# Two transposes of the last batch on TensorE, and three units one product later: a retention and Fourier-mixing block on one Trainium2 core

## The chip, the cores and the metric

The kernel runs on one core of one Trainium2 chip. The metric is the device time of one execution in microseconds. Before the change the median of 3 runs is 237.1 us (237.0 to 237.59). A difference of about 0.3% is what such a measurement can tell from none.

The core's engines run side by side, each through its own list of instructions: TensorE (PE in the profile, with its weight loads as PEld), VectorE (DVE), ScalarE (ACT), GpSimd (POOL) and SyncE (SP), whose queue here issues nearly all DMA. They wait for one another by semaphores.

## The reference

A retention layer over 4 batches, 8 heads, 768 steps and head size 64, and then a Fourier mixer with a feed-forward block of 512 to 2048 to 512:

```python
for t in range(S):
    state = gamma[None, :, None, None] * state + np.einsum('bhd,bhe->bhde', k[:, :, t], v[:, :, t])
    y[:, :, t] = scale * np.einsum('bhd,bhde->bhe', q[:, :, t], state)
...
x = np.ascontiguousarray(attn_out.transpose(0, 2, 1, 3)).reshape(B, S, H * D)
...
X = np.fft.fft(x, axis=1)
X = np.fft.fft(X, axis=2)
mixed = np.real(X).astype(np.float32)
u = x + mixed
mu = np.mean(u, axis=-1, keepdims=True)
var = np.mean((u - mu) ** 2, axis=-1, keepdims=True)
un = (u - mu) / np.sqrt(var + 1e-06)
ch = np.maximum(un @ w_ch1, 0.0) @ w_ch2
return (u + ch).astype(np.float32)
```

## The kernel before

The sequence of 768 is cut into six blocks of 128. Retention is computed by blocks for pairs of heads (four pairs a batch): products inside a block with a decay mask, and a state carried from block to block. The Fourier transforms are products with cosine and sine tables after folds. The feed-forward block runs on row blocks of 128 rows; its first product needs the normalised rows transposed.

**The order.** The work is written as small units in two strings of names, `FIRST` (batch 0 up to its first normalised rows, with the front of its feed-forward) and `LATER` (the rest, lines 49 to 95). The loop at line 1465 calls the units of `LATER` in turn through `held` (line 188), which ties each instruction to the one before it on the same engine:

```python
for n in range(n0, len(ins)):
    m = n - 1
    while m >= 0 and ins[m].engine != ins[n].engine:
        m -= 1
    if m >= 0:
        tc.add_manual_dep(ins[n], ins[m].name,
```

So the place of a name in the string is its place in the order of every engine that it uses, the DMA queue of SP among them. Semaphores and the banks of the PSUM pools are assigned by the compiler. `ps_g` (line 135) has five banks and serves nearly all intermediate products; the feed-forward products have a pool of three.

**The names that matter here.** The digits after the kind are mostly batch, then pair or row block, then part; a letter after @ is the engine that evacuates.

- `cq`, `ck`, `cv` (lines 477, 493, 504): GpSimd casts q, k and v of a pair to half precision, k with its decay. The loads `l`, `lq`, `lk`, `lv` are issued on SP.
- `s b i half` (`kv_unit`, line 728): three or two products of k and v on TensorE; block 0 is copied by ScalarE (L744), the others are added to the state by VectorE (L746), one after the other. It needs `ck` and `cv`.
- `t b i` (`t_unit`, line 666): TensorE transposes q (six blocks, L677) and, for pairs 0 and 1, k (six more); ScalarE copies q in two halves (L682) and k (L687). For pairs 2 and 3 the k transpose is a DMA. It needs `cq` and `ck`.
- `a b i part` (`a_unit`, line 703): two products of kT and qT (L712), evacuated by VectorE with the mask (L716) or by ScalarE in two activations (L722) with a GpSimd select behind them (L724).
- `y b i h` (L760, L763): the output of one head from qT, the state, the masked products and v.
- `c b rt rb3 part` (`ch_unit`, line 1200): four of the sixteen products of the second feed-forward layer of batch 0 (L1206); it needs the activations of its four hidden blocks.
- `r b rt` (`rstd_unit`, line 1134): ScalarE's square root (L1140) and VectorE's reciprocal (L1142) for three row blocks of batch 0, or two of a later batch. `r00` first computes the mean and variance of row block 0 on VectorE (L1015, L1016).
- `x b kb` (`s2_unit`): the last Fourier product of a row block (L1071), two ScalarE copies, and the sums on VectorE (L1078, L1087); `X` adds the input on GpSimd (L1110, L1112); `n` takes the statistics on VectorE (L1121, L1122); `u` writes the normalised rows `un` on ScalarE (L1130) or GpSimd.
- `U b kb @ engine` (`unT_unit`, line 1145): the transpose of `un` into `unT`. With @d it is one DMA transpose on SP (L1149). With @v or @a TensorE transposes four 128x128 blocks (L1153) into a bank of `ps_g` and VectorE or ScalarE copies them (L1154):

```python
if eng == "d":
    nc.sync.dma_start_transpose(unT[:, :, kb * P:(kb + 1) * P], un)
    return
```

- `H b g n` (`hp_unit`, line 1251): in batches 1 to 3 the first feed-forward product of two row blocks 2g and 2g+1 together (L1259), so it needs `unT` of both; the relu is L1164 on ScalarE or L1161 on VectorE.
- `j`, `p`, `q` (lines 1268, 1290, 1313): the second layer of such a pair of row blocks as seven products of halves (Strassen): sums of halves on VectorE (L1277), products `p` (L1308), and the additions `q` to the result (L1322), after which a row block is stored.

Of the kernel before, what the change touches and what calls it, by code (L numbers as in the profile page):

```python
# [51 lines left out]

|
i02 U01@v x04 X04 x03 i10 U02@a x05 i13 X05 i12 K0 cq10 Z c0000 c0001 i22 i20 i03 i11 X03 l10
l11 l12 i21 ck10 cv10 cq11 ck11 n04 u04@a c0002 n05 i23 n03 t10 c0020 s100 c0021 cv11 s101 t11
r00 a100@a c0010 a102@v a101@v l13 cq12 s110 ck12 c0011 u05@a a111@v u03@a c0022 a110@a y100
a112@v V10 y101 t12 lq20 s111 TB c0003 c0012 y110 U05@a cv12 s120 cq13 c0013 U04@v U03@a y111
ck13 t13 c0023 O01 pz00 w10 lk20 h016@a cv13 O00 a120@v a121@a pz01 s121 a122@a s130 h01C@a
h012@a s131 a132@v cq20 a131@a y121 h015@a lv20 lq21 lk21 a130@v y120 tq20 V00 ck20 tk20 h018@a
y131 y130 lv21 cv21 O02 cv20 h017@a h010@a h014@a h01F@a h01E@a h011@a h013@a h019@a ck21 V11  # L60
fs10 h01D@a fs11 h01A@a fd10 fd11 g10 fe10 fe11 z1 h01B@v c0100 pz10 V01 a201@v c0110 f110@a
f100@a w30 f101@a cq21 w11 pz11 lq22 lk22 lv22 f111@a gr12@a gr11@a lq23 lk23 c0101 g112 w20
a202@a r01 c0102 s200 c0103 tk21 gr10@v x11@v X11 x10@v n11 X10 c0111 c0112 tq21 x12@v n10 cq22
lv23 w31 s201 a200@a u11@a s210 c0120 c0121 c0122 u10@g gr13@a c0123 x13@v ck23 O03 y200 y201
c0113 tq22 U11@a X12 U10@v O05 n12 X13 ck22 w21 tk22 cv23 x15@v s211 cq23 r10 O04 a211@a H101@s
H105@s a212@a a210@v H106@a s230 x14@v cv22 n13 H102@s lq30 H103@a H100@a H107@a j10104 y210
# [19 lines left out]
p221 q221 j22204 p224 j22248 p225 p226 j22448 q225 j22404 j22304 u30@g U30@d gr30@a q226 p222  # L86
q222 X32 j22348 gr31@a x34@v p223 p227 q227 x33@v X33 q223 n33 H301@a x35@v H303@s H300@a H302@b
H305@s u33@a j30104 j30204 H304@a H306@a j30304 n32 r30 H307@b p301 q301 j30148 j30348 j30248
u32@a U32@d p304 U33@d j30448 p305 q305 j30404 p306 q306 X34 p302 q302 p303 q303 p307 H312@s
H317@a q307 H311@v n34 X35 n35 H315@a H313@s H316@v H310@a j31104 j31304 H314@b j31148 r31  # L90
j31248 p311 q311 j31204 j31448 j31404 j31348 p314 p315 q315 u35@a U35@d u34@g U34@d p316 q316
p312 q312 p313 q313 p317 q317 H325@b H324@v H326@s H322@b H321@b H320@s j32103 H323@a H327@s
j32136 j32236 p321 j32336 j32436 r32 j32168 j32368 p322 p324 j32268 p325 j32303 q321 j32203 p326
j32468 j32403 q325 p323 q326 q322 q323 p327 q327
# [1408 lines left out]
```

## Time and profile before

| | |
|---|---|
| median of 3 runs | 237.1 us |
| profiled execution, its own time | 237.41 us |
| its span, first to last instruction | 235.7 us |
| granted TensorE clock, mean | 0.996 |
| ScalarE relu of the first layer (L1164) | 117 instructions, 51.2 us |
| DMA share, SP queue (hardware_dynamic) | 67.5% of 16 engines over the span |
| transposes of `un` by DMA (L1149) | 15 |
| transposes of `un` by TensorE (L1153) | 32, eight row blocks |

A row of a timeline gives the start in us from the span's start, the duration, the engine, the line, the operation, out and in, shapes and a count of merged instructions; the bracket is the time that the engine sat idle before and who released it. Ends of products on TensorE are modelled, so that they overlap the next start; starts tell more. SPq is the SP queue issuing a DMA; a DMA row in the chain of waits runs from issue to landing.

### The profile page before, as it was taken

To read this page: it belongs to the slowest core of one execution; us is meant where nothing else is said; L and a number is where in the kernel's file an instruction comes from. 1 tells how busy PE (TensorE), PEld (TensorE's weight loads), DVE (VectorE), ACT (ScalarE), POOL (GpSimd) and SP (SyncE) were. 2 spreads that over 40 slices of the span, in tenths; PEclk is the share of its full clock that TensorE was granted. 3 is DMA by queue.
4 is the path that set the end of the run, shared out by engine and by line. 5 is a ranking of instruction groups with operands and counts; after the bars stand their busy time and mean duration, and the time that the engine had idled before them with its cause. 6 is when DMAs were issued, how large, how long until landed. Compare 5 with 4: busy or idle time off the path is not lost. (4 is left out here: it accounts for less than half of the span.)

```text
span 235.7 us, 6275 instructions
## 1 busy us (share of the span) xinstructions
PE 220.4 (94%) x2407; PEld 179.0 (76%) x2407; DVE 197.5 (84%) x491; ACT 150.5 (64%) x383; POOL 102.6 (44%) x176
## 2 busy tenths in 40 slices
PE   0888999989999999999999999999999999899993
PEld 0366778866675556889988999989799888788892
DVE  8799884878799989999999999889997987659473
ACT  5989758569998636795847847758537456041330
POOL 8378802576560399939007569441004341010000
PEclk9999999999999999999999999999999999999998
DMA  7999999999999999999997959942102420402202
GB/s 176 236 268 242 237 207 207 211 217 234 195 270 203 238 208 205 188 252 198 255 215 140 219 101 185 127 89 96 40 3 90 46 90 0 116 21 45 92 0 92
DMA packets 100958, 36.84 MB, mean 156 GB/s; under 512 B 91457, under 2 KB 97985, under 8 KB 100929
## 3 DMA queue, kind: packets, MB, share of 16 engines
q1 hardware_dynamic: 96704, 32.25, 67.5%
q0 software_dynamic: 4224, 4.19, 10.8%
q8 instruction: 19, 0.31, 0.6%
q14 instruction: 11, 0.08, 0.1%
HBM read 27.26 MB, written 6.29 MB: 142 GB/s over the span
## 5 line engine op out<-in xcount | busy, mean ns | idle before, releaser
L1164 ACT ACTIVATE ht<-psh 128x256 f16<-128x256 f32 (+2 forms) x117 | 51.2, 467 | 38.9 <-PE psh L1259 37.0
L1259 PE MATMUL psh<-unT,w 128*128 128x256 f16 x576 | 66.8, 273 | 1.1 <-DMA unT<-un 1.1
L1259 PEld LDWEIGHTS <-w 128*128 128x128 f16 x576 | 55.3, 98 | 7.9 <-DMA unT<-un 1.5
L1308 PEld LDWEIGHTS <-ht 128*128 128x128 f16 x440 | 41.5, 98 | 6.5 <-ACT ht L1164 1.3
L1110 POOL TENSOR_TENSOR u<-u,x 128x256 f32<-128x256 f32 x21 | 13.5, 643 | 36.6 <-DVE u L1078 24.9
L1308 PE MATMUL ps<-wide,ht 128*128 128x256 f16 x216 | 27.8, 273 | 0.1
L1277 DVE TENSOR_TENSOR ht<-ht 128x512 f16<-128x512 f16 (+2 forms) x57 | 23.8, 433 | 3.8 <-ACT ht L1164 3.3
L724 POOL TENSOR_SCALAR_AFFINE_SELECT atm<-atm 128x512 f16<-128x512 f16 x25 | 15.9, 650 | 18.7 <-issue 11.7
L1206 PE MATMUL psc<-w,ht 128*128 128x512 f16 x96 | 23.6, 379 | 0.0
L499 POOL TENSOR_SCALAR kd<-k,gexp 128x384 f16<-128x384 f32 x22 | 14.1, 650 | 16.2 <-PE ps L915 12.4
L746 DVE SCALAR_TENSOR_TENSOR s<-s,gk,wkK 128x128 f16<-128x128 f16 x48 | 16.2, 343 | 4.8 <-ACT s L744 3.2
L722 ACT ACTIVATE atm<-wkA 128x256 f16<-128x256 f32 x50 | 15.8, 395 | 5.3 <-PE wkA L712 5.1
L1308 PE MATMUL ps<-w,ht 128*128 128x256 f16 x144 | 18.7, 273 | 0.4 <-ACT ht L1164 0.4
L1322 DVE SCALAR_TENSOR_TENSOR ob<-ps,stats,u 128x256 f32<-128x256 f32 (+2 forms) x27 | 15.0, 562 | 3.3 <-PE ps L1308 3.3
L1161 DVE TENSOR_SCALAR ht<-psh 128x512 f16<-128x512 f32 (+2 forms) x19 | 10.7, 566 | 7.3 <-ACT ht L1164 3.5
L1121 DVE BATCH_NORM_STATS2 bst<-u 128x6 f32<-128x512 f32 x21 | 14.3, 682 | 2.3 <-POOL u L1112 2.3
L1130 ACT ACTIVATE un<-u,stats 128x512 f16<-128x512 f32 x18 | 13.0, 728 | 4.5 <-DVE stats L1122 4.5
L1322 DVE SCALAR_TENSOR_TENSOR u<-ps,stats,u 128x256 f32<-128x256 f32 (+2 forms) x27 | 15.0, 562 | 0.6 <-PE ps L1308 0.6
L508 POOL TENSOR_SCALAR v<-v 128x768 f16<-128x768 f32 x11 | 10.1, 925 | 11.5 <-DMA v<-in_v_dram 11.5
L1206 PEld LDWEIGHTS <-ht 128*128 128x128 f16 x96 | 8.8, 98 | 7.3
L1112 POOL TENSOR_TENSOR u<-u,x 128x256 f32<-128x256 f32 x21 | 13.7, 652 | 0.0
L770 ACT ACTIVATE x<-wkY,gexp 128x384 f16<-128x384 f32 x24 | 13.1, 589 | 0.7 <-PE wkY L763 0.6
(225 smaller groups left out, 458.3 us busy)
## 6 DMA issues: line engine op xcount, KB each, us to landing
out_dram<-ob SPq DMA_DIRECT2D x23, 256.0 KB, 2.9
k<-in_k_dram SPq DMA_DIRECT2D x14, 384.0 KB, 5.6
v<-in_v_dram SPq DMA_DIRECT2D x14, 384.0 KB, 6.2
q<-in_q_dram SPq DMA_DIRECT2D x12, 384.0 KB, 5.3
w<-in_moe_w_ch_dram POOLq DMA_DIRECT2D x8, 512.0 KB, 10.9
wide<-in_q_dram SPq DMA_DIRECT2D x4, 384.0 KB, 6.1
wide<-in_v_dram SPq DMA_DIRECT2D x2, 384.0 KB, 6.2
wide<-in_k_dram SPq DMA_DIRECT2D x2, 384.0 KB, 6.2
```

The lines of the kernel that those rows point to most:

```text
L499: nc.gpsimd.tensor_scalar(out=kd[:, :, h2, :], in0=k32[:, h2], scalar1=gkd[:, h0 + h2:h0 + h2 + 1], scalar2=1.0, op0=ALU.mult, op1=ALU.mult)
L722: nc.scalar.activation(dst[:, :, h2], wk[:, :, h2], AF.Copy, bias=0.0, scale=float(gam[2 * PAIR_ORDER[i] + h2] ** (-P)))
L724: nc.gpsimd.affine_select(out=dst, in_=dst, compare_op=ALU.is_ge, fill=0.0, base=0, pattern=[[0, 2], [0, 2], [1, P]], channel_multiplier=-1)
L746: nc.vector.scalar_tensor_tensor(out=s16[:, c], in0=s16[:, c - 1], scalar=gk2[:, hp:hp + 1], in1=wk[:, c - c0], op0=ALU.mult, op1=ALU.add)
L1112: nc.gpsimd.tensor_tensor(out=u[:, kb, 256:512], in0=u[:, kb, 256:512], in1=x[:, kb, 1, 257:1:-1], op=ALU.add)
L1121: nc.vector.bn_stats(bst, u[:, kb, :])
L1164: nc.scalar.activation(dst, src, AF.Relu, bias=0.0, scale=-1.0)
L1206: nc.tensor.matmul(psc_of[b, rb], ht16[:, fb, rb3 * P:(rb3 + 1) * P], w216[:, fb, :], start=(fb == 0), stop=(fb == NFB - 1))
L1259: nc.tensor.matmul(psh[:, t], w116[:, cb, fb * P:(fb + 1) * P], unT[:, cb, g * 256:(g + 1) * 256], start=(cb == 0), stop=(cb == 3))
L1277: nc.vector.tensor_tensor(out=out_, in0=x, in1=y, op=op)
L1308: nc.tensor.matmul(dst, lhsT, rhs[:, c0:c1], start=(n == 0 and (name is not None or k == 5 and m == 1)), stop=(n == 7), skip_group_check=True)
L1322: nc.vector.scalar_tensor_tensor(out=out_, in0=in_, scalar=r, in1=u_, op0=ALU.mult, op1=ALU.add)
```

## The change

Only the string `LATER` changes, in three places.

- Batch 1, first pairs: `s100` stands behind `c0021` instead of in front of it, and `t11` behind `c0010`, and with that also behind `r00` and `a100`, instead of in front of `r00`.
- Batch 2, first pair: `s200` stands behind `c0103` instead of in front of it.
- Batch 3: `U33` and `U35` are @v instead of @d: four transposes on TensorE and a copy on VectorE in place of a DMA transpose on SP. `U32` and `U34`, the other row blocks of the two pairs, stay DMA transposes.

```diff
-l11 l12 i21 ck10 cv10 cq11 ck11 n04 u04@a c0002 n05 i23 n03 t10 c0020 s100 c0021 cv11 s101 t11
-r00 a100@a c0010 a102@v a101@v l13 cq12 s110 ck12 c0011 u05@a a111@v u03@a c0022 a110@a y100
+l11 l12 i21 ck10 cv10 cq11 ck11 n04 u04@a c0002 n05 i23 n03 t10 c0020 c0021 s100 s101 cv11 r00
+a100@a c0010 t11 a102@v a101@v l13 cq12 s110 ck12 c0011 u05@a a111@v u03@a c0022 a110@a y100
...
-a202@a r01 c0102 s200 c0103 tk21 gr10@v x11@v X11 x10@v n11 X10 c0111 c0112 tq21 x12@v n10 cq22
+a202@a r01 c0102 c0103 s200 tk21 gr10@v x11@v X11 x10@v n11 X10 c0111 c0112 tq21 x12@v n10 cq22
...
-u32@a U32@d p304 U33@d j30448 p305 q305 j30404 p306 q306 X34 p302 q302 p303 q303 p307 H312@s
+u32@a U32@d p304 U33@v j30448 p305 q305 j30404 p306 q306 X34 p302 q302 p303 q303 p307 H312@s
...
-j31248 p311 q311 j31204 j31448 j31404 j31348 p314 p315 q315 u35@a U35@d u34@g U34@d p316 q316
+j31248 p311 q311 j31204 j31448 j31404 j31348 p314 p315 q315 u35@a U35@v u34@g U34@d p316 q316
```

## The prediction

> **What bounds the kernel now.** I read the page's busy table first, then a table of busy time by stretch, then TensorE's timeline from 48 us to the end looking only for gaps, and for each gap the timelines of the engines named as its releaser. (In the stretch rows the columns are the stretch, its length, busy us and instruction count of PE, PEld, DVE, ACT, POOL, then clock and DMA.)
>
> ```profile
> PE 220.4 (94%) x2407; PEld 179.0 (76%) x2407; DVE 197.5 (84%) x491; ACT 150.5 (64%) x383; POOL 102.6 (44%) x176
> ...
> 57.00:82.00 25.00, 25.00 (x266) 16.62 (x262) 22.96 (x55) 21.67 (x56) 10.92 (x17) 1.00 1.10 233
> 94.00:168.00 74.00, 73.73 (x835) 66.24 (x833) 69.40 (x171) 53.58 (x148) 38.36 (x61) 1.00 0.90 167
> ```
>
> TensorE sets the time: between 57 and 82 us it has no hole at all, between 94 and 168 us 0.27 us in 74. So a delay of TensorE at 57 us can't be made up by TensorE; it is carried until the next place where TensorE waits for something that has not been delayed too. The change touches three such places: 50 to 55 us, 82 to 91 us, and the last 40 us.
>
> **First place: s100 and t11 stand later.** TensorE before:
>
> ```profile
> 48.95 1.03 PE L1206 MATMUL psc<-w,ht 128*128 128x512 f16 x4
> 50.57 0.33 PE L739 MATMUL wkK<-v,kd 128*128 128x128 f16 x3 [0.59 <-POOL v L508]
> ...
> 52.50 0.51 PE L677 MATMUL tq<-ident,kd 128*128 128x128 f16 x6 [0.29 <-POOL kd L499]
> ...
> 54.37 0.33 PE L739 MATMUL wkK<-v,kd 128*128 128x128 f16 x3
> 54.53 1.03 PE L1206 MATMUL psc<-w,ht 128*128 128x512 f16 x4
> 55.40 0.38 PE L712 MATMUL wkA<-qTz,kT 128*128 128x256 f16 x2
> ```
>
> These are c0020, s100, the second half of t11, s110, c0011 and a111. Ends are modelled and overlap, so I count by starts: c0011 holds TensorE for 55.40 - 54.53 = 0.87 us. c0020 therefore left it free at 49.82, and s100 came 0.75 later because GpSimd's v cast was late. With c0021 between them (0.87, to 50.69) that hole is filled; with c0010 in front of t11 the 0.29 hole is filled too. Taken alone that is a gain of about 1.1 us.
>
> But t11 is more than its twelve transposes. It also issues three ScalarE copies (two for qT, one for kT), and these are moved past r00 and a100 on ScalarE. ScalarE and VectorE before:
>
> ```profile
> 51.27 0.27 ACT L744 CAST s<-wkK 128x128 f16<-128x128 f32 x1
> 52.25 1.61 ACT L682 COPY qTz<-tq 64x768 f16<-64x768 f16 x2 [0.70 <-PE tq L677]
> 53.88 0.80 ACT L687 COPY kT<-tq 128x768 f16<-128x768 f16 x1
> 54.58 0.30 ACT L1140 ACTIVATE stats<-stats,epsT 128x3 f32<-128x3 f32 x1
> 54.78 0.65 ACT L722 ACTIVATE atm<-wkA 128x256 f16<-128x256 f32 x2
> 55.30 0.28 ACT L744 CAST s<-wkK 128x128 f16<-128x128 f32 x1
> ```
>
> ```profile
> 51.58 1.56 DVE L746 SCALAR_TENSOR_TENSOR s<-s,gk,wkK 128x128 f16<-128x128 f16 x4 [1.16 <-ACT s L744]
> ...
> 53.78 0.18 DVE L1016 BATCH_NORM_AGGREGATE stats<-bst 128x2 f32<-128x6 f32 x1
> ```
>
> Each engine runs its instructions in the order of the list. r00's square root (L1140) reads the variance that VectorE aggregates until 53.78 + 0.18 = 53.96, behind the four state steps of s100 and s101, which begin when ScalarE's cast at 51.27 is done. Nothing of that moves: s100's products end at about 50.9 in the new order, so the cast stays at 51.27. Before, the copies of t11 ran while VectorE worked. Now ScalarE has nothing between 51.5 and the square root. I take 0.07 us for the hand-over: square root at 54.03, a100's two activations 0.20 later at 54.23, the copies 0.52 after that (55.30 - 54.78) at 54.75, kT 1.63 later (53.88 - 52.25) at 56.38, done 0.80 later at 57.18.
>
> Who waits: a111 needs kT and qT of that pair. It ran at 55.40; with the copies done at 57.18 it runs at about 57.25, **1.85 us later**. All that stands before it in the list (s110, c0011) is done by 56.0 even if s110 waits for the bank that a100's late evacuation frees at 54.9, so that wait adds nothing. The 1.1 us that TensorE gained are lost in front of a111, and 1.85 more. Bounds of this term: 1.5 if VectorE's chain comes 0.3 sooner, 2.2 if the square root and the copies don't overlap as before. I take 1.85: every duration in it is from these rows. What was cover (ScalarE's copies under VectorE's chain) is gone, and ScalarE, with 21.67 busy of 25.00 us behind it, can't give it back.
>
> **Second place: s200 behind c0103.** Here are the old TensorE, GpSimd and VectorE rows.
>
> ```profile
> 81.39 1.02 PE L1206 MATMUL psc<-w,ht 128*128 128x512 f16 x4
> 82.87 0.33 PE L739 MATMUL wkK<-v,kd 128*128 128x128 f16 x3 [0.46 <-POOL v L508]
> ...
> 83.90 0.63 PE L1071 MATMUL pq<-gk,g 128*128 128x129 f16 x8
> ...
> 91.17 0.19 PE L760 MATMUL wkY<-s,qTz 128*128 128x64 f16 x1 [0.19 <-DVE s L746]
> ```
>
> ```profile
> 80.31 2.51 POOL L508 TENSOR_SCALAR v<-v 128x768 f16<-128x768 f32 x2 [10.15 <-DMA v<-in_v_dram]
> ...
> 85.97 0.63 POOL L1110 TENSOR_TENSOR u<-u,x 128x256 f32<-128x256 f32 x1
> 86.56 0.63 POOL L1112 TENSOR_TENSOR u<-u,x 128x256 f32<-128x256 f32 x1
> ```
>
> ```profile
> 83.53 0.73 DVE L746 SCALAR_TENSOR_TENSOR s<-s,gk,wkK 128x128 f16<-128x128 f16 x2
> ...
> 84.81 0.48 DVE L1078 SCALAR_TENSOR_TENSOR u<-pq,g,qn 128x256 f32<-128x256 f32 x1 [0.24 <-ACT qn L1074]
> ...
> 87.23 0.69 DVE L1121 BATCH_NORM_STATS2 bst<-u 128x6 f32<-128x512 f32 x1 [0.76 <-POOL u L1112]
> ```
>
> The hole before s200 is 82.87 - 81.39 - 0.87 = 0.61 us; it ends with the cast of a v that came late by DMA. That cast goes by the loads, which the SP queue issues with several in flight, so I let it stay near 82.8. TensorE reaches s200 at 82.26 + 1.85 + 0.87 (c0103) = 84.98: no wait, **0.61 us back**, with or without the swap. Net so far +1.24.
>
> The swap has a price on VectorE: s200's two state steps stand in front of x11's sums. s200 is at 84.98 (before 82.87, +2.1), the sums follow at +1.85, at 86.66. Their first half ends at 87.14, GpSimd's two additions (0.59 apart by starts) run from 87.2, and the statistics that VectorE waits for start at about 88.47 instead of 87.23: **+1.24**, because GpSimd's chain behind the late v had slack there. That is TensorE's own delay, so the wait at 91.17 neither grows nor shrinks. Bounds: 0.61 given back at most, 0 if the v load slips as much as TensorE.
>
> **Third place: U33 and U35 by TensorE.**
>
> ```profile
> 199.16 1.20 SPq L1149
> ...
> 200.41 4.45 DMA unT<-un
> ...
> 203.18 1.04 PE L1308 MATMUL ps<-wide,ht 128*128 128x256 f16 x8
> 204.91 7.16 PE L1259 MATMUL psh<-unT,w 128*128 128x256 f16 x64 [0.69 <-DMA unT<-un]
> ...
> DMA to landing us min/median/max: 2.4/2.5/4.8
> ```
>
> The first row is U32's issue, the second U33's transfer behind it on the SP queue. H31x needs both. TensorE was free at 203.18 + 0.87 = 204.05 and started at 204.91: 0.86 us. U32 alone lands about 2.5 after its issue, near 201.7, far ahead. So the hole goes. In exchange TensorE does four transposes for U33, four for U35:
>
> ```profile
> 92.55 0.61 PE L1153 MATMUL pst<-ident,un 128*128 128x128 f16 x8
> 93.00 0.39 PE L1071 MATMUL pq<-gk,g16r 128*128 128x129 f16 x4
> ...
> L1154 DVE COPY unT<-pst x4: 418/422/425, 35.7 to 108.7; 128x512 f16<-128x512 f16 x4
> ```
>
> Eight take 0.45 us of TensorE, so each group 0.22. Neither waits for its operand:
>
> ```profile
> 196.07 0.72 ACT L1130 ACTIVATE un<-u,stats 128x512 f16<-128x512 f32 x1
> ...
> 212.57 0.71 ACT L1130 ACTIVATE un<-u,stats 128x512 f16<-128x512 f32 x1
> 214.78 1.05 PE L1308 MATMUL ps<-wide,ht 128*128 128x256 f16 x8
> ...
> 201.67 0.41 DVE L1277 TENSOR_TENSOR s4t<-ht 128x512 f16<-128x512 f16 x1
> ```
>
> un of block 3 is there at 196.79, of block 5 at 213.28, before TensorE's places (about 199.7 and 214.78). VectorE's copy (0.42, some 0.35 by starts) pushes the sum at 201.67 to end near 202.43; p303, which reads it, moves from 202.31 to 202.53 by the transposes: still in time by 0.1. **-0.86 + 0.22 + 0.22 = -0.42 us.** Bounds: -0.64 if U35's group finds a hole, -0.2 if p303 and the sums behind U35's copy each slip 0.1.
>
> [...]
>
> **Sum.** +1.85 - 0.61 - 0.42 = +0.82 us. The profiled execution took 237.41 us (span 235.7, 1.71 around it), so it would be 238.2; the median of the runs, 237.1, is 0.3 lower and becomes **237.9**.
>
> **The rivals.**
> 1. The v load slips with TensorE, nothing comes back at s200: +1.85 - 0.42, **238.5**. For it: loads and output stores share the SP queue, and stores wait for VectorE's delayed results. Against: the loads run several deep.
> 2. The transposes don't overlap: each takes the modelled 0.22 us of one (0.61 less seven steps of 0.056), 1.75 in all instead of 0.44: **239.2**. Against: the row of eight. [...]
> 3. The copies of t11 are no later than before: VectorE's aggregate comes while ScalarE is busy, as it did. Then TensorE arrives early at s200, waits for the same cast at 82.8, and the statistics at 87.23 hold it at 91.17 as before: the front gain is lost, the end gain kept, **236.7**.
> 4. As 3, and the loads move ahead as well, since GpSimd casts q and k of the next pairs earlier: the 1.1 us of the first place pass through to the end, **235.6**, faster. It decides if the two v casts end by 81.7 instead of 82.82. Against: a load's place depends on DMA that is full (share 1.10 above).
> 5. VectorE or ScalarE give up slack between 94 and 168 us and TensorE closes 0.27 us of holes there and some of the end's: **237.2**.
>
> **How the numbers follow.** Forecast 0.56 (own range 237.4 to 238.5), rival 1 0.13, 2 0.03, 3 0.08, 4 0.13, 5 0.07. 0.3% (0.71 us) is about what a measurement of this kernel can tell from no change, so slower begins at 237.81 and the forecast lies just above it: two thirds of its chance, 0.37, with 1 and 2 makes slower 0.54; a third of it with 3 and 5 makes 0.33 within; faster 0.13. The range leaves out rival 4 and rival 2: 236.4 to 238.9.
>
> **What would show it.** In the changed profile: no POOL wait before s100, t11 and s200; ScalarE idle from about 51.5 to 54 in front of L1140, released by VectorE; a111 at about 57.2 after a hole that is put down to ScalarE's kT copy (L687); s200 at about 85; H31x with no DMA wait; thirteen unT transposes on SP instead of fifteen. Wrong if a111 starts before 55.4, or if VectorE's aggregate ends well before 53.9.

## The result, and the profile after

| | before | changed |
|---|---|---|
| median of 14 runs each, same chip | 237.0 us (235.74 to 237.88) | 238.56 us (237.6 to 240.82) |
| ratio, 95% interval | | 1.0072 [1.0043, 1.0102] |
| profiled execution, its own time (span) | 237.41 us (235.7) | 237.66 us (236.0) |

The changed kernel is slower by 0.7%, 1.56 us by the medians; 237.9 had been forecast, with a range of 236.4 to 238.9. The two profiled executions lie only 0.25 us apart, so the loss must not be read off this pair alone: the one of before was slow among its own kind, the changed one fast among its own. The page of the changed kernel has this busy table:

```profile
PE 220.4 (93%) x2415; PEld 179.4 (76%) x2415; DVE 198.7 (84%) x493; ACT 150.5 (64%) x383; POOL 103.0 (44%) x176
```

TensorE has the eight transposes more and is as busy as before. The first place, on the timeline of TensorE:

```profile
50.66 0.44 PE L739 MATMUL wkK<-v,kd 128*128 128x128 f16 x5
51.41 0.39 PE L712 MATMUL wkA<-qTz,kT 128*128 128x256 f16 x2 [0.31 <-ACT kT L687]
...
54.88 0.34 PE L739 MATMUL wkK<-v,kd 128*128 128x128 f16 x3 [1.10 <-ACT atm L722]
55.05 1.03 PE L1206 MATMUL psc<-w,ht 128*128 128x512 f16 x4
57.19 0.39 PE L712 MATMUL wkA<-qTz,kT 128*128 128x256 f16 x2 [1.11 <-ACT kT L687]
```

The first row is s100 and s101 together, with no wait for GpSimd; a100 now waits 0.31 for its own kT copy, which t11 had covered. Then come two holes of 1.1 us by the brackets (1.27 by starts): s110 waits for the bank that a100's ScalarE evacuation frees, and a111 (57.19) waits for t11's kT. Who holds ScalarE up is on its own timeline and on VectorE's:

```profile
51.25 0.27 ACT L744 CAST s<-wkK 128x128 f16<-128x128 f32 x1
53.98 0.30 ACT L1140 ACTIVATE stats<-stats,epsT 128x3 f32<-128x3 f32 x1 [2.45 <-DVE stats L1016]
54.18 0.64 ACT L722 ACTIVATE atm<-wkA 128x256 f16<-128x256 f32 x2
54.71 1.60 ACT L682 COPY qTz<-tq 64x768 f16<-64x768 f16 x2
56.34 0.80 ACT L687 COPY kT<-tq 128x768 f16<-128x768 f16 x1
```

```profile
53.76 0.18 DVE L1016 BATCH_NORM_AGGREGATE stats<-bst 128x2 f32<-128x6 f32 x1
```

ScalarE sits idle for 2.45 us in front of the square root, which VectorE's aggregate releases at 53.94. Everything behind it in the list waits with it, though a100's activations and t11's copies need nothing from VectorE. The second place, TensorE and then GpSimd:

```profile
84.95 0.33 PE L739 MATMUL wkK<-v,kd 128*128 128x128 f16 x3
...
92.24 0.19 PE L760 MATMUL wkY<-s,qTz 128*128 128x64 f16 x1 [0.19 <-DVE s L746]
```

```profile
81.25 2.18 POOL L508 TENSOR_SCALAR v<-v 128x768 f16<-128x768 f32 x2 [9.61 <-DMA v<-in_v_dram]
```

s200 (84.95) comes after both v casts (83.43) and doesn't wait; TensorE stands 1.07 us behind the profile of before at 92.24 (91.17 there). The last 45 us on TensorE, and the group of DMA transposes on SP:

```profile
191.41 1.05 PE L1259 MATMUL psh<-unT,w 128*128 128x256 f16 x8
...
200.38 0.39 PE L1153 MATMUL pst<-ident,un 128*128 128x128 f16 x4
200.60 0.60 PE L1308 MATMUL ps<-cd,ht 128*128 128x256 f16 x4
...
204.10 1.04 PE L1308 MATMUL ps<-wide,ht 128*128 128x256 f16 x8
204.97 7.15 PE L1259 MATMUL psh<-unT,w 128*128 128x256 f16 x64
...
214.79 0.39 PE L1153 MATMUL pst<-ident,un 128*128 128x128 f16 x4
215.01 1.04 PE L1308 MATMUL ps<-wide,ht 128*128 128x256 f16 x8
...
218.50 7.15 PE L1259 MATMUL psh<-unT,w 128*128 128x256 f16 x64
```

```profile
L1149 SPq DMA_TRANSPOSE unT<-un x13: 1190/1216/2652, 105.1 to 210.4; - x13
```

Each group of four transposes takes 0.22 us from its start to the next product's. H31x (204.97) follows 0.87 behind p307: its hole is gone.

### The profile page after: what moved, and what is told of

It reads as the page before. It is cut to its first block, busy times and chain, and to the rows that moved or that the text cites. A ratio compares the mean times of both kernels' runs of the same rounds, so it can differ in the third digit from the quotient of the medians.

```text
span 236.0 us, 6285 instructions
## 1 busy us (share of the span) xinstructions
PE 220.4 (93%) x2415; PEld 179.4 (76%) x2415; DVE 198.7 (84%) x493; ACT 150.5 (64%) x383; POOL 103.0 (44%) x176
## 5 line engine op out<-in xcount | busy, mean ns | idle before, releaser
L499 POOL TENSOR_SCALAR kd<-k,gexp 128x384 f16<-128x384 f32 x22 | 14.8, 682 | 14.8 <-PE ps L915 12.2
```

Of the source, the lines that this page charges most:

```text
L499: nc.gpsimd.tensor_scalar(out=kd[:, :, h2, :], in0=k32[:, h2], scalar1=gkd[:, h0 + h2:h0 + h2 + 1], scalar2=1.0, op0=ALU.mult, op1=ALU.mult)
```

## The experiments

All were timed in five rounds beside the kernel before on the same chip. They fall into four sets; the median of the kernel before was 236.3 to 236.4 in the three sets on one chip and 236.9 in the set on another. The 84 executions of it in these sets lie between 235.5 and 238.7, with a median of 236.5, so a single profiled execution says little of a change of 1 us.

**One part at a time.** First, only the order at the first place, `s200` and both `U` as before:

```diff
-n03 t10 c0020 s100 c0021 cv11 s101 t11
-r00 a100@a c0010 a102@v
+n03 t10 c0020 c0021 s100 s101 cv11 r00
+a100@a c0010 t11 a102@v
```

> Only the first place of the change: s100 behind c0021, t11 behind c0010 and with that behind r00 and a100; s200, U33 and U35 as before. Theory (t11's ScalarE copies wait behind r00's square root, which waits for VectorE): a111 at 57.2 us instead of 55.4, of that 0.6 to 0.8 given back before 92 us where TensorE no longer waits for the late v, so 1.1 to 1.2 us slower than before in the profile. The end keeps its waits: H31x 0.7 to 0.9 us for the DMA of U33. Rival (the moves themselves gain, the loss comes from the transposes or from s200): 0.5 to 1.1 us faster than before.

Measured: 238.03 us, ratio 1.0063 [1.0041, 1.0085]. On its TensorE timeline the two holes are those of the changed kernel, and H31x still waits for its DMA, by 0.40 us where 0.7 to 0.9 had been expected (the last row is cut off at 210 us by the view):

```profile
54.99 0.34 PE L739 MATMUL wkK<-v,kd 128*128 128x128 f16 x3 [1.10 <-ACT atm L722]
...
57.30 0.39 PE L712 MATMUL wkA<-qTz,kT 128*128 128x256 f16 x2 [1.11 <-ACT kT L687]
```

```profile
205.23 4.98 PE L1259 MATMUL psh<-unT,w 128*128 128x256 f16 x44 [0.40 <-DMA unT<-un]
```

Nearly the whole loss comes from the first place. Then only s200 behind c0103:

```diff
-r01 c0102 s200 c0103
+r01 c0102 c0103 s200
```

> Only s200 behind c0103, the rest as before. Theory (the place is pinned by the late v load through GpSimd's additions and VectorE's statistics): the 0.6 us hole in front of s200 goes, and comes back in front of the state products at 91 us; total within 0.3 us of before. Rival (TensorE's hole is the limit): 0.5 to 0.6 us faster.

Measured: 236.52 us, ratio 1.0007 [0.9985, 1.003]. In its profile s200 goes without a wait, and nothing is gained. In this execution there was nothing to gain: the v casts end at 81.69 us (79.63 and 2.06), and c0102 holds TensorE from 81.36 to 82.23, so the old place would have had no hole either. Then only U33 and U35 on TensorE:

```diff
-p304 U33@d j30448
+p304 U33@v j30448
...
-u35@a U35@d u34@g
+u35@a U35@v u34@g
```

> Only U33 and U35 by TensorE, the order of the rest as before. Theory: the 0.86 us in front of H31x goes, 2 x 0.22 us of transposes come: 0.4 us faster. Rival (a group of four transposes between long products costs 0.9 us): 0.9 us slower.

Measured: 236.38 us, ratio 0.9992 [0.9975, 1.0009]; the 0.42 us of the forecast (0.18%) lies inside that interval, and so does zero. Its profile is worth more than its time, because up to 199 us its order is that of before, in an execution whose loads came early. First TensorE, then GpSimd:

```profile
55.30 0.38 PE L712 MATMUL wkA<-qTz,kT 128*128 128x256 f16 x2
...
81.28 1.02 PE L1206 MATMUL psc<-w,ht 128*128 128x512 f16 x4
82.15 0.33 PE L739 MATMUL wkK<-v,kd 128*128 128x128 f16 x3
...
203.12 7.15 PE L1259 MATMUL psh<-unT,w 128*128 128x256 f16 x64
...
216.66 7.15 PE L1259 MATMUL psh<-unT,w 128*128 128x256 f16 x64
```

```profile
79.48 2.06 POOL L508 TENSOR_SCALAR v<-v 128x768 f16<-128x768 f32 x2 [9.80 <-DMA v<-in_v_dram]
```

In the old order, s200 stands 0.87 behind c0102 here: **no hole**. The v casts start at 79.48, not 80.31, and end at 81.54, before TensorE comes. The hole of 0.61 us in the profile of before came from a load that landed later in that execution. Beside this profile the changed kernel's a111 is 1.89 later (57.19 less 55.30), H31x 1.85 (204.97 less 203.12), the last feed-forward products 1.84 (218.50 less 216.66), and the span 1.9 (236.0 less 234.1). Here the loss of the first place runs through to the end whole.

**Is it the square root?** The changed kernel with r00 behind t11's copies; ScalarE's order alone differs:

```diff
-cv11 r00
-a100@a c0010 t11 a102@v
+cv11
+a100@a c0010 t11 r00 a102@v
```

> The changed kernel with r00 alone moved behind t11; TensorE's, VectorE's and GpSimd's order is that of the changed kernel, only ScalarE runs the copies before the square root. Theory: the copies start when t11's transposes end (about 52.8), kT is there by about 55.3, a111 runs before 55.4 instead of at 57.2, and the late v load holds what is gained: 0.7 to 1.3 us faster than the changed kernel, 0.3 to 0.9 us faster than the kernel before. Rival (the loss of the changed kernel is not r00's wait): the same time as the changed kernel, 0.5 to 1.5 us above before.

Measured: 236.56 us, ratio 1.0014 [0.9997, 1.0031]. The loss is gone; the gain over before that I had expected did not come. ScalarE's rows of this kernel:

```profile
54.33 1.61 ACT L682 COPY qTz<-tq 64x768 f16<-64x768 f16 x2 [0.54 <-PE tq L677]
55.97 0.80 ACT L687 COPY kT<-tq 128x768 f16<-128x768 f16 x1
56.66 0.30 ACT L1140 ACTIVATE stats<-stats,epsT 128x3 f32<-128x3 f32 x1
```

The copies now wait for t11's own transposes on TensorE, and the square root for nothing. In this execution the k of t10 was late and TensorE waited 1.33 us for it, so its times can't be set beside the others', but the distance from s100 to a111 can:

```profile
52.43 0.44 PE L739 MATMUL wkK<-v,kd 128*128 128x128 f16 x5
...
56.82 0.39 PE L712 MATMUL wkA<-qTz,kT 128*128 128x256 f16 x2 [0.72 <-ACT kT L687]
```

That is 4.39 us. In the changed kernel it is 6.53 (50.66 to 57.19), in the profile of before 4.83.

The same from the other side: the square root stays in front, but the mean and variance are computed before the state steps of s100 (`BN` names the unit that r00 otherwise calls first):

```diff
-n03 t10 c0020 c0021 s100
+n03 t10 BN c0020 c0021 s100
```

> The changed kernel with one thing moved on VectorE: the mean and variance of row block 0, which r00 computes first, stand in front of s100's state steps; every other engine runs the order of the changed kernel. Theory: the variance is there at 51.4 us instead of 53.9, r00's square root follows ScalarE's cast without a wait, t11's copies start behind t11's own transposes at about 52.9, kT at 55.3, a111 at 55.4 to 55.9 instead of 57.2: 1.0 to 1.7 us faster than the changed kernel, within 0.6 us of the kernel before. Rival (ScalarE's order itself costs the time, or the t11 transposes come too late on TensorE): no faster than the changed kernel.

Measured: 236.56 us, ratio 0.9995 [0.9971, 1.0018]. ScalarE's rows, then TensorE's (here too the k of t10 was late, by a wait of 1.02 us):

```profile
52.72 0.27 ACT L744 CAST s<-wkK 128x128 f16<-128x128 f32 x1 [0.87 <-PE wkK L739]
52.88 0.30 ACT L1140 ACTIVATE stats<-stats,epsT 128x3 f32<-128x3 f32 x1
```

```profile
52.35 0.44 PE L739 MATMUL wkK<-v,kd 128*128 128x128 f16 x5
...
56.73 0.39 PE L712 MATMUL wkA<-qTz,kT 128*128 128x256 f16 x2 [0.72 <-ACT kT L687]
```

The square root follows the cast with no wait, a111 comes 4.38 us behind s100, and the loss is gone again, with the order of ScalarE and TensorE that lost 0.7%. Two edits on two engines that share only this wait both remove the loss.

**Dose.** The changed kernel with the mean and variance of row block 0 computed twice in front of that square root, so that the same wait is longer:

```diff
 if b == 0 and rt == 0:
-    bn_unit(0)()
+    bn_unit(0)(); bn_unit(0)()
```

> The changed kernel with the mean and variance of row block 0 computed twice, one behind the other, ahead of r00's square root (some 0.5 to 0.7 us more on VectorE). If ScalarE's copies of t11 stand behind that square root as I say, the square root moves from 53.98 to 54.5-54.7, a111 from 57.19 to 57.7-57.9, and the time rises by 0.5 to 0.7, to 238.6-238.9 at full clock, with the clock of 0.993 in a quarter of the executions or more, since the hole ahead of s110 grows to 1.6-1.8 us. If the wait for VectorE is not on the path, the time stays at 238.1.

Measured: 239.73 us, ratio 1.0124 [1.0092, 1.0157]; the changed kernel in the same rounds (below) 238.88. Its ScalarE and then TensorE:

```profile
51.46 0.27 ACT L744 CAST s<-wkK 128x128 f16<-128x128 f32 x1
54.98 0.30 ACT L1140 ACTIVATE stats<-stats,epsT 128x3 f32<-128x3 f32 x1 [3.25 <-DVE stats L1016]
```

```profile
58.19 0.61 PE L712 MATMUL wkA<-qTz,kT 128*128 128x256 f16 x2 [1.11 <-ACT kT L687]
```

The square root is 1.00 later than in the changed kernel, a111 exactly as much, 58.19 less 57.19 (0.21 of it is there before VectorE's added work: the cast that releases VectorE stands at 51.46, not 51.25). The other 0.79 is the work on VectorE, for which 0.5 to 0.7 had been expected. The three executions with a clock above 0.995 have a median of 238.76, against 238.09 for those of the changed kernel in the same rounds: 0.67 us more, from three executions on each side.

**Where would a gain be?** t11 back in its old place, c0021 still in front of s100, the rest as changed:

```diff
-s101 cv11 r00
-a100@a c0010 t11 a102@v
+s101 cv11 t11
+r00 a100@a c0010 a102@v
```

> The changed kernel with t11 back in front of r00, so that only s100 has moved in the first place (c0021, s100, s101, t11, r00, a100, c0010). Theory: the hole in front of s100 is filled, but t11's k transposes still wait for GpSimd's cast at 52.4, so the 0.7 us come back there and a111 stays at 55.4: the time of the kernel before, less at most 0.4 for the transposes at the end. Rival (filling the hole gains): 0.7 to 1.1 us faster than before.

Measured: 236.89 us, ratio 1.0001 [0.9983, 1.0019]. And with c0010 in front of t11, both in front of r00:

```diff
-s101 cv11 r00
-a100@a c0010 t11 a102@v
+s101 cv11 c0010
+t11 r00 a100@a a102@v
```

> The changed kernel with c0010 in front of t11 and t11 in front of r00 and a100 (c0021, s100, s101, c0010, t11, r00, a100). Theory: both holes are filled and ScalarE's copies keep their old place at 52.3, kT at 54.7, a111 at about 54.7 instead of 55.4 of before; the late v load holds part of it: 0.4 to 1.1 us faster than before. Rival (the place is pinned by the loads alone): the time of before.

Measured: 236.66 us, ratio 1.0004 [0.9983, 1.0025]. 0.4 to 1.1 us had been expected. Its TensorE has a111 only 0.22 earlier than before, and then a wait that the profile of before did not have there:

```profile
55.18 0.38 PE L712 MATMUL wkA<-qTz,kT 128*128 128x256 f16 x2
...
78.38 0.39 PE L712 MATMUL wkA<-qTz,kT 128*128 128x256 f16 x2 [0.40 <-DMA kT<-kd]
```

Neither beats the kernel before. In this profile the hole before s100 is filled, but t11's k transposes still wait 0.21 for GpSimd's cast, and s110 waits 0.33 for t11's qT copy, which it did not before. Of the little that TensorE won at 55 us, part went to the next DMA that landed late. Whether the loads bound the time so in general was not tried.

**The clock.** The changed kernel once more, for its spread:

> The changed kernel itself, timed beside the others and for a second profile. Theory: 1.3 to 1.8 us above before; in the profile a111 at 57.2 and VectorE as the releaser of ScalarE's 2.4 us in front of the square root again; the place of the late v cast near 80 differs by some tenths from the first profile, since it goes by the loads. Rival (the loss is that of one placement on one chip): within 0.5 us of before.

Measured: 238.07 us, ratio 1.0069 [1.0042, 1.0096]. Its profiled execution took 239.62 us and shows something that the first did not. Windows of the changed kernel's first profile, then of this one (columns as in the prediction; the clock is the last but two):

```profile
54.00:57.40 3.40, 1.42 (x9) 0.68 (x10) 1.42 (x4) 3.35 (x8) 2.51 (x4) 1.00 1.23 244
58.40:60.80 2.40, 2.40 (x40) 1.86 (x38) 1.71 (x5) 2.23 (x8) 1.37 (x2) 1.00 1.34 228
```

```profile
54.00:57.40 3.40, 1.21 (x8) 0.48 (x7) 1.53 (x4) 3.14 (x7) 2.27 (x4) 1.00 1.24 250
58.40:60.80 2.40, 2.40 (x20) 1.59 (x19) 0.50 (x1) 1.23 (x4) 0.13 (x1) 0.50 1.37 225
```

Behind the two holes TensorE's granted clock is 0.50, and it does 20 products in 2.4 us instead of 40. On its timeline a111 is where it should be, and t12 (the last row) comes at 61.24:

```profile
57.42 0.39 PE L712 MATMUL wkA<-qTz,kT 128*128 128x256 f16 x2 [1.11 <-ACT kT L687]
...
61.24 0.50 PE L677 MATMUL tq<-ident,q16z 128*128 128x128 f16 x6
```

From a111 to t12 it is 3.82 us here and 2.17 in the first profile (57.19 to 59.36, from the same view), 1.65 more. To tell whether the holes do that, I filled them: ten products with a zero operand, which add nothing to a sum that is open there, five in front of s110 and five in front of a111. In the profile below, ScalarE's square root still waits 2.46 us for VectorE and starts at 54.01.

```diff
-cq12 s110 ck12 c0011 u05@a a111@v
+cq12 FZ s110 ck12 c0011 u05@a FZ a111@v
...
+def zero_products():
+    for _ in range(5):
+        nc.tensor.matmul(psc_of[0, 1], qts[0][0:D, 1, 0], w216[0:D, 0],
+                         start=False, stop=False)
```

> The changed kernel with ten added products of a zero operand (0.22 us each), five ahead of s110 and five ahead of a111, which add nothing to the sum of c001x: TensorE works through its two holes of 1.10 and 1.11 us while every wait of the other engines stays. It separates the wait itself from the clock. If the clock drop is caused by the holes (busy 1.2 to 1.4 of 3.4 us), no execution shows a mean granted clock of 0.993, where 7 of 25 of the changed kernel so far did; a111 still starts between 57.1 and 57.5 us, so the fastest executions stay at 237.6 or above and the median falls by at most 0.4, to 237.7-238.0 (ratio to before 1.004 to 1.006). If the drop has nothing to do with the holes (a state of the chip), about 3 of 12 executions still show 0.993. If the wait was not the loss at all, the time is that of before, 236.5.

The changed kernel in the same rounds:

> The changed kernel once more, on the same chip and in the same rounds as the two before it: 238.0 to 238.5, ratio to before 1.005 to 1.009, a clock of 0.993 in 2 to 5 of 12 executions, each of these near 239.7. If the earlier drops were the chip's own, none here.

And the filled one again, for the count:

> The changed kernel with its two holes filled by zero products, once more, for the count: so far 0 of its 6 executions show a mean granted clock of 0.993, against 10 of 31 of the changed kernel itself. If the holes cause the drop, none of these either, and the median lies at 237.7-238.4, ratio 1.005 to 1.009, since the wait for the square root is still there. If the drop comes by chance of the chip, a third of the executions show it, and the median is above 238.5.

Measured: filled 238.27 us, ratio 1.0089 [1.0058, 1.0119], and again 238.3, 1.0074 [1.0048, 1.01]; the changed kernel once more 238.88, 1.0108 [1.0064, 1.0151], above its expected 238.5 because three of its six executions have the lower clock. Filled, windows and TensorE:

```profile
54.00:57.40 3.40, 3.40 (x19) 1.27 (x18) 1.39 (x4) 3.34 (x8) 2.05 (x4) 1.00 1.01 185
58.40:60.80 2.40, 2.40 (x40) 1.88 (x39) 1.70 (x5) 2.21 (x8) 1.32 (x2) 1.00 1.08 239
```

```profile
56.05 1.25 PE L1437 MATMUL psc<-w,qTz 64*128 64x512 f16 x5
57.23 0.39 PE L712 MATMUL wkA<-qTz,kT 128*128 128x256 f16 x2
```

TensorE is busy all through, and a111 starts where it did: the product waits for its operand whether the engine idles or not. In the table all executions stand by their mean granted clock. (A mean of 0.996 has nothing to do with the holes: the profile of before has it too, and its clock is 0.50 from about 234 us on, behind the last product, 1.8 of 235.7 us.)

| kernel | executions | clock 0.993 or less | median of these | median of the rest |
|---|---|---|---|---|
| before (experiments' sets) | 84 | 0 | | 236.54 us |
| changed, three sets | 31 | 10 | 239.66 us | 237.95 us |
| holes filled, two sets | 12 | 0 | | 238.27 us |
| statistics twice | 6 | 3 | 240.43 us | 238.76 us |
| first place alone | 6 | 0 | | 238.03 us |
| the six others without both holes | 72 | 0 | | 236.4 to 236.9 us |

If filling made no difference, a split as uneven as 10 of 31 against 0 of 12 would come up about once in forty times (exact test on the four counts, 0.02). Filling the holes does not lower the time of the executions at full clock (238.27 against 237.95); none of the 12 shows the lower clock. The first place alone has both holes and shows none in 6, which at the rate of 10 in 31 happens once in ten; counted with the changed kernel it makes 10 of 37, and the split against 0 of 12 then comes up by chance about once in 24 times. That was not followed up.

## Why the prediction was right, and where its sizes were off

**First place, +1.85: right, row by row.** Square root forecast for 54.03, measured 53.98 (the hand-over from VectorE, put at 0.07 us, took 0.04: 53.94 to 53.98); copies 54.75 and 54.71; kT 56.38 and 56.34; a111 57.25 and 57.19. That the wait for the variance is the cause, and not the later place of t11 as such, is shown by two edits that remove only that wait and by one that lengthens it. Against the cleaner execution of the old order the term is 1.89. That the edit had to lose all that TensorE won at 50 us and more was in the rows of before.

**Second place, -0.61: there in some executions and not in others.** The prediction took "The hole before s200 is 82.87 - 81.39 - 0.87 = 0.61 us" and gave it back. That s200 would go without a wait, at 84.98, was right (84.95). But the hole goes by a load, and the prediction booked it from one profile: in the profile of the old order with only U33 and U35 changed it is not there, and in that of s200 moved alone there would have been none. What isn't lost before can't be given back after; without the term the sum is that of rival 1, +1.85 - 0.42 = +1.43.

The times have both. Taken set by set, at full clock, the changed kernel is 0.9 us above before in the result's own set (237.9 against 237.0, 10 and 14 executions) and 1.0 in the set on the other chip (237.88 against 236.86), near the sum of +0.82. On the chip where before has 236.3 to 236.4 it is 1.8 (238.09 against 236.32, three executions only), and 1.6 for the first place alone. What differs between sets is the kernel before, not the changed one. That the hole before s200 is the difference would fit; it isn't shown, since only one profile of before was taken. So the sum fits the result's own set in part by luck: its base and its hole came from the same slow executions of before, and the third term is too small for these times to resolve.

Rival 1's reason was another: a v load that slips with TensorE so that s200 waits as before; in the profile s200 doesn't wait. The +1.24 forecast for 92 us was 1.07 by this pair of profiles: VectorE's statistics, forecast for 88.47, start at 88.30.

**Third place, -0.42: the parts as forecast, the sum not resolved.** Each group of transposes costs 0.22 (200.38 to 200.60, 214.79 to 215.01), and H31x's hole is gone. Two rows of before that the prediction did not need, from TensorE's timeline:

```profile
190.71 1.05 PE L1259 MATMUL psh<-unT,w 128*128 128x256 f16 x8 [0.38 <-DMA unT<-un]
...
218.28 7.15 PE L1259 MATMUL psh<-unT,w 128*128 128x256 f16 x64
```

The changed kernel lags by 0.70 us at 191 us (191.41 against 190.71), by 0.06 at H31x (204.97 against 204.91) and by 0.22 at H32x (218.50 against 218.28). So 0.64 is won up to H31x, its own 0.86 less 0.22, and 0.22 is paid behind it: -0.42. (At 92 us the lag was still 1.07. The 0.37 between were given back in front of 190.71, where this profile of before waits 0.38 for another DMA transpose and the changed one doesn't; the prediction had no term for that.) Measured alone it is 0.9992 [0.9975, 1.0009]. Rival 2, transposes that do not overlap, is out: it has 1.75 us for the eight, and these rows show 0.44, though the profile models 0.22 us (219 ns) for each single one.

**What the prediction did not have: the clock.** The 10 of 31 executions with a mean clock of 0.993 are 1.7 us longer than the rest (239.66 less 237.95). That lifts the mean of the changed kernel by about 0.55 us. Of the 14 executions of the result four are such: the median is 238.56 with these and 237.9 without, 0.66 us apart, as much as that result lies above the forecast. The prediction looked at the holes as time lost and never at what TensorE's clock makes of them.

Rivals 3 and 4 needed copies no later than before; the wait of 2.45 us ends them. For 5, the old and new order against each other at 55, 203 and 217 us (1.89, 1.85, 1.84) show 0.05 us given up in between; against the profile of before it is 0.37 more, at 190 us, as said above.

## What to carry to other kernels

Before a unit is moved, list every instruction that it issues on each engine, and ask what it is moved behind: an engine works its list in order, so a copy that needs nothing waits with the square root in front of it, here for 2.45 us. Before a hole in one profile is booked as time to win or to get back, look whether it is there in a second execution: holes in front of freshly loaded data came and went here by a load's arrival (0.61 us in front of s200 in the profile of before, none in that with only U33 and U35 changed). And price a hole on TensorE twice, once as waiting and once for the clock of what comes behind it: here a111 came 1.79 and 1.89 us later than in the two profiles of the old order, and the executions with the lower clock are another 1.7 us longer.

## What was not expected of the hardware

Behind the same two holes of 1.1 us the clock fell in some executions and not in others: 10 of 31 of the changed kernel have a mean granted clock of 0.993, the others 0.996 or more. In its second profile, with TensorE busy for 1.21 of the 3.4 us from 54.0 to 57.4, the clock is 0.50 from 57.7 to 61.2 us, 3.4 us long (from the means of the stretches around it: 0.67 from 57.4 to 58.4, 0.50 to 60.8, 0.94 to 64). In its first profile (busy for 1.42) and in that of the first place alone (1.30) it stays at 1.00. With a longer hole (1.89 and 1.11 us in the profile with the statistics computed twice) 3 of 6 executions have the lower clock; in that profile it is 0.50 from 57.1, still inside the second hole, to 63.9, 6.8 us long, and its mean over the span is 0.982. In the 3.4 us ahead of each drop TensorE was busy for 1.5 us in both profiles, by the rows of its timeline.

The second drop is twice as long as the first, 6.8 us against 3.4. From 50 us on, the longest idle stretch ahead of the second is 1.9 us (2.1 by starts), ahead of the first 1.1 (1.27 by starts), and TensorE worked between the two holes. What decides from one execution to the next whether the clock falls was not shown, and how little work is too little was not tried. A single hole of 1.0 to 1.4 us stands in three other profiles, in front of t10's k transposes (1.33 us with r00 behind t11, 1.02 with the statistics early, 1.36 with t11 in its old place). The eight products behind it take 1.72, 1.73 and 1.72 us by starts, as the same eight do in the changed kernel (1.73), and the mean clocks of these executions are 1.0, 0.996 and 0.999; three executions don't say that it always is so.
